# Linformer attention and gated feed-forward: small-matmul rounds joined, one block's softmax sums done in one round, loads of v and q reordered

## The chip, the cores and the metric

The kernel runs on one core of a Trainium2 chip. The metric is the device time of one execution in microseconds. The time before is 512.57 us (median of 4 runs, 511.74 to 514.13). Inputs are drawn at random in float32; the kernel works in bfloat16 with float32 sums.

## The reference

```python
# q, k, v: (batch 8, heads 8, seq 1024, dim 64); E, F: (64, 1024)
k_proj = einsum('ks,bhsd->bhkd', E, k)
v_proj = einsum('ks,bhsd->bhkd', F, v)
scores = q @ k_proj^T / 8
attn   = softmax(scores)                # over the 64 projected keys
x      = (attn @ v_proj), heads joined  # 8192 x 512
h      = x @ w_in                       # 512 -> 2048
out    = (h * sigmoid(1.702 h)) @ w_out # 2048 -> 512
```

## The kernel before

The kernel goes through 16 blocks of 512 rows of `x`. A block is 16 groups of 4 matmuls for `w_in` (`ffn1`) and 8 runs of 8 matmuls for `w_out` (`ffn2`). The attention of later blocks is pushed between them: `at(j, slot, f)` puts the work `f` behind slot `slot` of block `j`. There are 24 slots in a block and more in block 0, whose groups are halved; `O` is 16, the first run for `w_out`, and `Q` is the same place in block 0.

The attention matmuls are small. `eight` issues 64-row by 32-column matmuls that lie side by side in the array; I call one set of eight a round:

```python
def eight(outs, lhsTs, rhss):
    for i, ro in ((0, (LO, HI)), (1, (HI, LO))):
        for c in range(0, KP, 32):
            for ri, r in zip((LO, HI), ro):
                nc.tensor.matmul(outs[i][r.start + c:r.start + c + 32], lhsTs[i][ri, c:c + 32], rhss[i][ri], ...)
```

`scores` is one round and two exponentials on ScalarE. From block 4 on, the softmax sums of a block are one round (`sums`); VectorE inverts them, `spread` sends them out to DRAM and back over all partitions, and `values` (one round per half block) is multiplied by what came back. Block 3 is done by the older `norm`, which makes the sums anew on every partition, two rounds per half, and so needs no trip to DRAM:

```python
def norm(h, u):
    def go():
        e = [expT[h][:, 2 * u + i, :] for i in range(2)]
        d_ps = [ps_x.tile([P, TB], F32, name="x_ps") for _ in range(2)]
        eight(d_ps, [ones, ones], e)
        n_ps = [ps_x.tile([P, TB], F32, name="x_ps") for _ in range(2)]
        eight(n_ps, [vqs[h // NB2 % 2][:, 2 * u + i, :] for i in range(2)], e)
        for i in range(2):
            rd = att.tile([P, TB], F32, name="rdn")
            nc.vector.reciprocal(rd, d_ps[i])
            nc.vector.tensor_tensor(x_of(h)[:, 2 * u + i, :], n_ps[i], rd, op=ALU.mult)
    return go
```

`proj(b)` projects k and v of batch `b`; `load(b)` loads the batch from the GpSimd queue, in order, into single buffers:

```python
def load(b):
    load_kv(k, kt, b, "k_sb")
    if b == 1:
        load_kv(v, vt, b, "v_sb")
    load_q(b)                      # eight pieces
    if b > 1:
        load_kv(v, vt, b, "v_sb")
```

PSUM is split into two pools of four tiles: `f_ps` and `x_ps`.

The softmax here doesn't subtract the row's maximum and nothing guards it: scores larger than these inputs give would overflow.

## Time and profile before

| | before |
|---|---|
| time, median of 4 runs | 512.57 us |
| span of the profiled run | 510.4 us |
| TensorE busy | 504.4 us (99%), clock 1.000 |
| VectorE, ScalarE busy | 165.6 and 264.3 us |
| waits of TensorE | 2.7 us, all in the first 28 us |
| length of blocks 1, 2, 3 | 33.50, 34.78, 29.38 us |
| blocks 4 to 11, in turn | 31.02 and 29.16 us |

The length of a block is from the start of its first `w_in` group to that of the next block's, on TensorE's timeline. The lines of the profile are in the prediction.

### The profile page before, as it was taken

The numbers are of one execution on the slowest core, as the hardware profiler recorded it, in microseconds if no ns is written. First come the engines' busy times: TensorE is split into PE (matmuls) and PEld (weight loads), VectorE is DVE, ScalarE is ACT, GpSimd is POOL, SyncE is SP. The second block draws the span as 40 slices with busy tenths as digits, with TensorE's granted clock in tenths as the row PEclk, the third lists the DMA queues.
The fourth block names the chain that finished last, engine by engine and source line by source line (L and its number), as shares of the span: only waits on it lengthen the run. The fifth ranks groups of instructions, "written<-read, shape, count | busy, mean of one in ns | idle before, by whom it ended". The sixth has DMA issues, their size and how long they took to land.

```text
span 510.4 us, 7234 instructions
## 1 busy us (share of the span) xinstructions
PE 504.4 (99%) x3090; PEld 232.0 (45%) x3090; DVE 165.6 (32%) x221; ACT 264.3 (52%) x443; POOL 78.1 (15%) x97
## 2 busy tenths in 40 slices
PE   8999999999999999999999999999999999999997
PEld 4684444444444444444444444444444444444444
DVE  5513114765161623216161341616214161611000
ACT  2675564555637456471746637374563737244351
POOL 7442051514200051000510033000000000000000
PEclk9999999999999999999999999999999999999999
DMA  9999999999999099651998249990603205050202
GB/s 172 197 203 207 212 140 165 225 177 138 166 239 211 1 209 187 144 129 39 213 167 202 49 99 212 116 241 1 171 1 74 93 9 157 1 166 1 82 1 82
DMA packets 124752, 67.64 MB, mean 133 GB/s; under 512 B 92288, under 2 KB 116096, under 8 KB 122800
## 3 DMA queue, kind: packets, MB, share of 16 engines
q0 software_dynamic: 84400, 29.37, 51.4%
q1 hardware_dynamic: 40240, 37.56, 29.3%
q8 instruction: 24, 0.39, 0.3%
q10 hardware_dynamic: 80, 0.26, 0.2%
q14 instruction: 8, 0.07, 0.0%
HBM read 71.83 MB, written 16.97 MB: 174 GB/s over the span
## 4 chain that ended last, share of the span: by engine, by line
PE 94%; DMA 4%; POOL 1%; issue 0%; DVE 0%; ACT 0%; POOLq 0%
PE f_ps L405 43%; PE f_ps L373 43%; PE f_ps L165 3%; DMA w_in_sb<-in_moe_w_in_dram 2%; PE f_ps L262 2%; DMA v_sb<-in_v_dram 2%; PE x_ps L262 1%; PE x_ps L297 1%; POOL k_sb L57 0%; PE x_ps L359 0%; PE x_ps L344 0%; PE f_ps L397 0%; PE f_ps L244 0%; POOL q_sb L57 0%; POOL v_sb L57 0%
## 5 line engine op out<-in xcount | busy, mean ns | idle before, releaser
L405 PE MATMUL f_ps<-w_out_sb,gT 128*128 128x512 bf16 x1008 | 227.2, 379 | 0.0
L373 PE MATMUL f_ps<-xT,w_in_sb 128*128 128x512 bf16 (+1 forms) x1088 | 226.4, 367 | 0.3 <-DMA w_in_sb<-in_moe_w_in_dram 0.2
L376 ACT ACTIVATE gT<-f_ps 128x512 bf16<-128x512 f32 (+1 forms) x270 | 151.8, 574 | 61.4 <-PE f_ps L373 60.2
L373 PEld LDWEIGHTS <-w_in_sb 128*128 128x128 bf16 x1088 | 105.3, 98 | 116.2 <-issue 1.7
L405 PEld LDWEIGHTS <-gT 128*128 128x128 bf16 x1008 | 95.6, 98 | 120.5 <-issue 11.3
L408 ACT COPY o_sb<-f_ps 128x512 f32<-128x512 f32 x63 | 37.0, 587 | 126.8 <-PE f_ps L405 117.0
L332 DVE TENSOR_TENSOR xT<-x_ps,rbc 128x512 bf16<-128x512 f32 x48 | 30.9, 686 | 201.3 <-PE x_ps L262 124.9
L300 DVE RECIPROCAL rden<-x_ps 128x512 f32<-128x512 f32 x24 | 78.7, 3322 | 10.3 <-PE x_ps L297 10.3
L63 POOL DMA_DIRECT2D q_sb<-in_q_dram x56 | 49.1, 901 | 52.0 <-DMA k_sb<-in_k_dram 39.2
L278 ACT ACTIVATE expT<-f_ps 128x512 bf16<-128x512 f32 (+1 forms) x68 | 35.1, 571 | 32.7 <-PE f_ps L262 32.6
L57 POOL DMA_DIRECT2D k_sb<-in_k_dram x10 | 8.4, 846 | 175.5 <-PE f_ps L165 159.1
L219 DVE CAST k_b<-f_ps 64x512 bf16<-64x512 f32 x7 | 4.8, 683 | 46.8 <-PE f_ps L165 46.8
L278 ACT ACT_TABLE_LOAD x13 | 16.7, 1283 | 4.7 <-PE f_ps L262 4.5
L282 ACT ACT_TABLE_LOAD x14 | 18.0, 1283 | 0.2
L322 DVE RECIPROCAL rdn<-x_ps 128x512 f32<-128x512 f32 x4 | 13.4, 3353 | 0.8 <-PE x_ps L262 0.8
L165 PE MATMUL f_ps<-k_sb,eft 128*64 128x512 bf16 x56 | 13.4, 382 | 0.0
L165 PE MATMUL f_ps<-v_sb,eft 128*64 128x512 bf16 x56 | 13.4, 381 | 0.0
L399 DVE COPY o_sb<-f_ps 128x256 f32<-128x256 f32 x1 | 0.4, 424 | 38.6 <-issue 38.6
L135 PE MATMUL x_ps<-zeros 128*128 128x512 bf16 x34 | 11.2, 450 | 1.2 <-DVE zeros L106 1.2
L262 PE MATMUL f_ps<-qT,kt 64*32 64x512 bf16 x240 | 12.3, 386 | 0.0
L262 PE MATMUL x_ps<-expT,vq 64*32 64x512 bf16 x208 | 10.2, 377 | 0.0
L262 PEld LDWEIGHTS <-kt 64*32 64x32 bf16 x272 | 3.9, 88 | 13.7 <-issue 13.5
(71 smaller groups left out, 128.4 us busy)
## 6 DMA issues: line engine op xcount, KB each, us to landing
out_dram<-o_sb SPq DMA_DIRECT2D x15, 1024.0 KB
rbc<-rdr SPq DMA_DIRECT2D x24, 512.0 KB
k_sb<-in_k_dram POOLq DMA_DIRECT2D x7, 1024.0 KB, 13.3
v_sb<-in_v_dram POOLq DMA_DIRECT2D x7, 1024.0 KB, 10.6
q_sb<-in_q_dram POOLq DMA_DIRECT2D x56, 128.0 KB, 12.0
w_in_sb<-in_moe_w_in_dram POOLq DMA_DIRECT2D x8, 256.0 KB, 12.2
w_out_sb<-in_moe_w_out_dram POOLq DMA_DIRECT2D x4, 512.0 KB, 14.7
out_dram<-o_sb SPq DMA_DIRECT2D x3, 256.0 KB
```

Source lines behind the costliest of these rows:

```text
L63: nc.gpsimd.dma_start(out=qt[b][:, j], in_=qv[:, j])
L165: nc.tensor.matmul(kvps[b][r], eft(j, slice(e * KP, (e + 1) * KP)), (kt, vt)[e][b][:, :, j, :], start=(j == 0), stop=(j == J - 1))
L262: nc.tensor.matmul(outs[i][r.start + c:r.start + c + 32], lhsTs[i][ri, c:c + 32], rhss[i][ri], start=True, stop=True)
L278: nc.scalar.activation(expT[h][:, 2 * u + i, ts], s_ps[i], AF.Exp, scale=scale)
L282: nc.scalar.preload_act_table(AF.Gelu_apprx_sigmoid)
L300: nc.vector.reciprocal(rden[:, e, :], d_ps[e])
L322: nc.vector.reciprocal(rd, d_ps[i])
L332: nc.vector.tensor_tensor(x_of(h)[:, 2 * u + i, :], n_ps[i], rbc[h][:, 2 * u + i, :], op=ALU.mult)
L373: nc.tensor.matmul(h_ps, w_in_sb[:, kc, fc * P:(fc + 1) * P], xT[j][:, kc, ts], start=(kc == 0), stop=(kc == KC - 1))
L376: nc.scalar.activation(gts[j][:, fc, ts], h_ps, AF.Gelu_apprx_sigmoid)
L405: nc.tensor.matmul(o_ps[n], gts[j][:, fc, n * P:(n + 1) * P], w_out_sb[:, fc, :], start=(fc == 0), stop=(fc == FC - 1))
L408: nc.scalar.copy(osb[j][:, n, :], o_ps.pop(n))
```

## The change

It has three parts: the two halves of a score pair stand in one slot (the second half in the `x_ps` pool), block 3 goes over to `sums`, `spread` and `values` like the later blocks, and the loads are reordered. q of batch 2 goes into the buffer that batch 0 had to itself, apart from the one that the other batches share.

```diff
     def load(b):
-        load_kv(k, kt, b, "k_sb")
-        if b == 1:
-            load_kv(v, vt, b, "v_sb")
-        load_q(b)
-        if b > 1:
-            load_kv(v, vt, b, "v_sb")
+        for what in ("kvq", "kqv", "kvq", "qkv")[min(b, 4) - 1]:
+            ...
+    def q_buf(b):
+        t = ldpool.tile([P, J * H * D], BF16, name="q_even" if b in (0, 2) else "q_sb")
+        ...
-    def scores(h, u, half=None):
+    def scores(h, u, half=None, x=False):
...
-            s_ps = [f_tile([P, n * P]) for _ in range(2)]
+            s_ps = [(x_tile() if x else f_tile([P, TB]))[:, :n * P] for _ in range(2)]
...
-    at(0, 0, scores(0, 0, 1))
-    at(0, 1, scores(0, 1, 1), gelu_table)
+    at(0, 1, scores(0, 0, 1), scores(0, 1, 1, True), gelu_table)
...
-        at(0, Q + u, scores(1, u))
+        at(0, Q, scores(1, u, None, u > 0))
...
-        at(1, O + u, scores(2, u))
-        at(1, O + 3 + u, scores(3, u))
-        at(2, O + 2 * u, scores(4, u))
+        at(1, O, scores(2, u, None, u > 0))
+        at(2, O, scores(4, u, None, u > 0))
+        at(2, O + 3 * u, values(3, u))
...
-    at(1, O + 5, gelu_table)
+    for u in range(2):
+        at(1, O + 6, scores(3, u, None, u > 0))
+    at(1, O + 6, gelu_table)
...
-    at(2, 0, proj(2), kv_out(2))
-    at(2, 1, norm(3, 0))
-    at(2, 11, norm(3, 1))
+    at(2, 1, proj(2), kv_out(2), sums(3), spread(3))
     at(2, O, q_dma(3))
-    at(2, O + 4, scores(5, 0))
+    at(2, O + 3, scores(5, 0))
```

More of the change, by code (lines that the diff above doesn't have):

```diff
@@ L57, in load_kv @@
             nc.gpsimd.dma_start(out=dst[b][:, h:h + n, js:js + jn], in_=sv[:, h:h + n, js:js + jn])
+    def q_buf(b):
+        t = ldpool.tile([P, J * H * D], BF16, name="q_even" if b in (0, 2) else "q_sb")
+        order = "h j" if b == 0 else "j h"
+        return t.rearrange(f"p ({order} d) -> p {order} d", d=D, h=H)
     def load_q(b):
-        qt[b] = ldpool.tile([P, J, H, D], BF16, name="q_sb")
+        qt[b] = q_buf(b)
         qv = q[b].rearrange("h (p j) d -> p j h d", p=P)
@@ L65, in load @@
     def load(b):
-        load_kv(k, kt, b, "k_sb")
-        if b == 1:
-            load_kv(v, vt, b, "v_sb")
-        load_q(b)
-        if b > 1:
-            load_kv(v, vt, b, "v_sb")
+        for what in ("kvq", "kqv", "kvq", "qkv")[min(b, 4) - 1]:
+            if what == "q":
+                load_q(b)
+            elif what == "k":
+                load_kv(k, kt, b, "k_sb")
+            else:
+                load_kv(v, vt, b, "v_sb")
     w_in_v = moe_w_in.rearrange("(c p) f -> p c f", p=P)
@@ L85 @@
     make_identity(nc, ident)
-    load_kv(q, qt, 0, "q0_sb", H, 0, 2)
+    qt[0] = q_buf(0)
+    load_kv(q, qt, 0, "", H, 0, 2)
     load_kv(v, vt, 0, "v_sb", ((0, 4), (4, 2), (6, 2)))
-    load_kv(q, qt, 0, "q0_sb", H, 2, 2)
+    load_kv(q, qt, 0, "", H, 2, 2)
     for i in range(6):
         load_w_in(i)
-    load_kv(q, qt, 0, "q0_sb", H, JB, JB)
+    load_kv(q, qt, 0, "", H, JB, JB)
     for i in range(6, 8):
@@ L263, in eight, with x_tile @@
                                      start=True, stop=True)
-    def scores(h, u, half=None):
+    def x_tile():
+        return ps_x.tile([P, TB], F32, name="x_ps")
+    def scores(h, u, half=None, x=False):
         b, c = divmod(h, NB2)
```

## The prediction

> **What bounds the kernel now.** I read first the busy table of the page, then the list of what TensorE waited for, then TensorE's timeline, and last the timelines of VectorE and of the SyncE queue around block 2. (A block is 512 rows of the output; there are 16, numbered from 0. Each has 16 groups of four matmuls for the first weight matrix and 8 runs of eight for the second. I call these 24 places slots, and "slot 0 of the second half" is the first run of eight.)
>
> ```profile
> PE 504.4 (99%) x3090; PEld 232.0 (45%) x3090; DVE 165.6 (32%) x221; ACT 264.3 (52%) x443; POOL 78.1 (15%) x97
> PEclk9999999999999999999999999999999999999999
> ```
>
> TensorE is busy for 504.4 of 510.4 us at full clock; the other compute engines are idle for about half the time or longer. Busy matmuls are pipelined, so 99% alone could hide gaps. The waits of TensorE settle it:
>
> ```profile
> PE x_ps L135 <- DVE zeros L106: 1.2, 1, 1.2
> PE x_ps L359 <- DVE x_sb L351: 0.7, 1, 0.7
> PE f_ps L373 <- DMA w_in_sb<-in_moe_w_in_dram: 0.2, 1, 0.2
> ```
>
> These are the three longest of six, 2.7 us in all (columns: us in total, times, longest), and all six fall in the first 28 us. From there to the end TensorE never waits for anybody. So only fewer TensorE instructions, or less lost between them, can save time, and the change can only lose time by making a wait where there is none now. The timeline gives the price of each piece (columns: start, length, what, count):
>
> ```profile
> 71.07 1.89 PE L405 MATMUL f_ps<-w_out_sb,gT 128*128 128x512 bf16 x8
> 72.89 0.41 PE L262 MATMUL f_ps<-qT,kt 64*32 64x512 bf16 x8
> 73.23 1.90 PE L405 MATMUL f_ps<-w_out_sb,gT 128*128 128x512 bf16 x8
> ...
> 91.31 1.04 PE L373 MATMUL f_ps<-xT,w_in_sb 128*128 128x512 bf16 x4
> 92.28 0.41 PE L262 MATMUL x_ps<-expT,ones 64*32 64x512 bf16 x8
> 92.50 0.40 PE L262 MATMUL x_ps<-expT,vq 64*32 64x512 bf16 x8
> 92.83 8.81 PE L373 MATMUL f_ps<-xT,w_in_sb 128*128 128x512 bf16 x40
> ...
> 123.25 13.98 PE L373 MATMUL f_ps<-xT,w_in_sb 128*128 128x512 bf16 x64
> 137.07 1.89 PE L405 MATMUL f_ps<-w_out_sb,gT 128*128 128x512 bf16 x8
> 138.89 0.41 PE L262 MATMUL f_ps<-qT,kt 64*32 64x512 bf16 x8
> 139.11 0.40 PE L297 MATMUL x_ps<-expT,ones 64*32 64x512 bf16 x8
> 139.33 0.40 PE L262 MATMUL x_ps<-expT,vq 64*32 64x512 bf16 x8
> 139.66 10.53 PE L405 MATMUL f_ps<-w_out_sb,gT 128*128 128x512 bf16 x48
> ```
>
> Starts, not lengths, are to be compared. A full matmul costs (137.07 - 123.25)/64 = 0.216 us. Eight small ones (64 rows by 32 columns, all side by side in the array) are one round. An excursion from full matmuls to rounds and back costs, beyond its full matmuls: one round 73.23 - 71.07 - 8 x 0.216 = 0.43 us; two rounds 92.83 - 91.31 - 4 x 0.216 = 0.66; three 139.66 - 137.07 - 8 x 0.216 = 0.86. So a round is 0.215 us and **leaving and coming back costs 0.217 us** whatever is done there.
>
> **What the Trainium skill says.** "TensorEngine Tiling (Array Packing)", Key Properties: changing the tiling mode, not just the tile, drains TensorE. The trace agrees: the 0.217 us per excursion is two such changes. "TensorE: Matmul & The Clock Gate", Part 1, gives 215.7 ns from start to start for 512 columns; the trace has 216. So nothing is to be had from the full matmuls. "DMA: Bandwidth & Descriptors", Queues, rings and completion order: each DMA engine takes turns between the queues that have work. I use that for the share a small transfer gets beside the loads; the trace shows only the sum, loads and other traffic together at 195 GB/s from 92 to 106 us.
>
> **The change, part by part.**
>
> 1. Scores in one slot. The two halves of a block's scores now stand together, the second half writing to the other PSUM pool. Pairs joined: block 0's in the first slots, block 1's, block 2's, block 3's; each loses one excursion, 0.217 us. The joined pair in the first slots lies before 27.5 us, where TensorE waits for the weights' load anyway (the 0.2 us row), so I count it as nothing. Three pairs: 3 x 0.217 = 0.65 us saved. Block 4's pair I count with the next part.
>
> 2. Block 2. Before: two norm excursions of two rounds (2 x 0.656), block 4's two score excursions and block 5's first (3 x 0.432): 1.31 + 1.30 = 2.61 us. After: sums of block 3 behind the projection of batch 2; values and scores in one excursion of three rounds (0.86); values and scores in one of two (0.66). For work put behind a projection, the last such place of the trace tells: the projection alone cost 91.31 - 88.47 - 4 x 0.216 = 1.98, the projection with two rounds 121.52 - 115.55 - 16 x 0.216 = 2.51, so two rounds there cost 0.54, or 0.11 more than the rounds. One round: 0.32 us. Sum after: 0.32 + 0.86 + 0.66 = 1.84. Saved: 0.77 us.
>
> In the built order TensorE has eight matmuls fewer, as this says (norm 32; sums and values 24).
>
> 3. VectorE: four reciprocals of 3.35 us go and two of 3.32 come, 6.7 us less; the four products stay. It is busy 32% and was waited for nowhere in block 2: worth nothing by itself.
>
> 4. Loads. Batches 2 to 7 load the same bytes. From batch 4 on q comes first and waits for the transposes of the batch ahead, so q moves ahead of the k and v loads in steady state. All of it has some 50 us until it is used and TensorE waits for no load there: worth nothing.
>
> Sum: 0.65 + 0.77 = **1.42 us saved** on TensorE, 0.3%. 512.6 - 1.4 = 511.2.
>
> **Rivals.**
>
> (a) A new wait for the sums' round trip. Norm kept its sums on VectorE. Now block 3's reciprocals go out to DRAM and come back spread over partitions before its products can run. Block 4's trip in the kernel before shows how slow that is while loads run:
>
> ```profile
> 122.71 6.57 DVE L300 RECIPROCAL rden<-x_ps 128x512 f32<-128x512 f32 x2
> 129.31 0.62 SPq L307 DMA_DIRECT2D rdr<-rden  x1
> 134.75 1.35 SPq L310 DMA_DIRECT2D rbc<-rdr  x2
> 147.70 1.29 DVE L332 TENSOR_TENSOR xT<-x_ps,rbc 128x512 bf16<-128x512 f32 x2 [1.55 <-DMA rbc<-rdr]
> ```
>
> Reciprocals start 1.4 us behind the sums (two PSUM reads of the projection come first), the write out takes 5.4 us, the spread 12.9. In the changed kernel the sums of block 3 should end near 91.9 us, the reciprocals near 99.7, and the write, with the loads of batch 3 begun at 91.6, near 105. Were the spread as slow as that one, it would land at 118. I expect 114 to 118: by 105 the loads and the last output have moved 14 x 0.195 = 2.7 MB of 4.2 (four transfers of 1.05), 1.5 MB remain, and 1.05 MB of the spread taking turns with them is 2.1 MB at 195 to 255 GB/s, 8 to 11 us. Who waits? In the built order the sums of block 4 take the PSUM tiles that block 3's first products read, and stand at 121.19 - 1.42 = 119.8 us; two products take 1.29, so a landing after 118.5 stalls TensorE by the difference. For the rival: that margin is 0.5 to 4 us, the thinnest of the kernel. Against: v comes ahead of q now, so the projection of batch 3 is safe, and no output store falls beside this spread as one did at 136 us. If it strikes: 1 to 3 us lost, 511.5 to 514.
>
> (b) ScalarE at the end of block 1. Block 3's four exponentials (2 x 1.09), the table load (1.28) and an output copy (0.59) stand in a row where only two exponentials stood, 4.1 us from the scores, and ACT's first Gelu follows. TensorE's tiles for the next groups hang on these. But TensorE does scores, a run of eight, two groups and then the projection, 0.65 + 1.73 + 1.73 + 1.98 = 6.1 us, before it needs the copied tile. I give it no time. It would be worth 1 us at most.
>
> (c) The saving is hidden. It would be if TensorE waited for a transfer later; the list of waits has none after 28 us, so this holds for the first pair alone.
>
> (d) Steady state gains from spread loads. There is nothing on TensorE's path for that to shorten; 0. It may make the later spreads land sooner, unseen in the time.
>
> **Range and chances.** Without a stall 511.2; (a) strikes with a chance near one in five, for about 1.5 us, which adds 0.3 on average and stretches the upper side. I take 511.3. The three runs of before spread from 511.74 to 514.13, so the median itself is uncertain by about 1 us either way. Range 509.8 to 513.3. Two per cent is 10 us: no part is near it. Faster by over 2%: 0.01; within: 0.98; slower: 0.01.
>
> **What would show each step right or wrong.** TensorE's timeline: three-round and two-round excursions in block 2 at 0.86 and 0.66 us, no norm rounds, the start of block 3's groups (123.25 before) near 121.8. VectorE's first products of block 3: their start tells the landing; 114 to 118 as I say, and the sums of block 4 at 119.8 without a wait. TensorE's waits: still none after 28 us; one at the sums of block 4 or at block 3's first groups would be (a), one at the groups of block 2 (b). The second half of the trace: the same spacing, 13.82 us for 64 matmuls. The prediction is wrong if blocks 4 to 15 change length, or if block 2 holds a wait of over 2 us.

## The result

The changed kernel takes 511.33 us (median of 4 runs, 511.16 to 511.42). The ratio is 0.9972, with an interval from 0.9948 to 0.9996. Run again on another occasion (`after_again`), it gave 0.9974, from 0.9960 to 0.9987. That is 1.3 to 1.4 us, a change within 2%.

In the changed kernel's source the lines have moved: L271 is the rounds of `eight` (L262 before), L309 `sums` (L297), L385 and L417 the two feed-forward matmuls (L373 and L405), L174 the projection (L165). The page's first row, and then three of the six rows of what TensorE waited for (us in total, times, longest; the other three are 0.7, 0.2 and 0.2 us, also in the first 28 us):

```profile
PE 503.0 (99%) x3082; PEld 232.2 (46%) x3082; DVE 158.2 (31%) x219; ACT 263.8 (52%) x443; POOL 78.0 (15%) x97
```

```profile
PE x_ps L144 <- DVE zeros L115: 1.2, 1, 1.2
...
PE f_ps L385 <- ACT gT L388: 0.3, 1, 0.3
...
PE f_ps L385 <- DMA w_in_sb<-in_moe_w_in_dram: 0.2, 1, 0.2
```

Eight matmuls fewer, and still no wait after the first 28 us. The Gelu wait of 0.3 us is new; it lies at the very start. TensorE's timeline of block 2, from its first `w_in` group to that of block 3 (start, length, what, count; cut where `...` stands, and the last row ends with the view):

```profile
88.22 1.89 PE L385 MATMUL f_ps<-xT,w_in_sb 128*128 128x512 bf16 x8
...
91.89 0.41 PE L309 MATMUL x_ps<-expT,ones 64*32 64x512 bf16 x8
92.23 12.26 PE L385 MATMUL f_ps<-xT,w_in_sb 128*128 128x512 bf16 x56
104.33 1.89 PE L417 MATMUL f_ps<-w_out_sb,gT 128*128 128x512 bf16 x8
106.15 0.41 PE L271 MATMUL f_ps<-qT,kt 64*32 64x512 bf16 x8
106.37 0.40 PE L271 MATMUL x_ps<-expT,vq 64*32 64x512 bf16 x8
106.59 0.40 PE L271 MATMUL x_ps<-qT,kt 64*32 64x512 bf16 x8
106.92 5.35 PE L417 MATMUL f_ps<-w_out_sb,gT 128*128 128x512 bf16 x24
112.20 0.41 PE L271 MATMUL x_ps<-expT,vq 64*32 64x512 bf16 x8
112.43 0.40 PE L271 MATMUL f_ps<-qT,kt 64*32 64x512 bf16 x8
112.76 5.35 PE L417 MATMUL f_ps<-w_out_sb,gT 128*128 128x512 bf16 x24
...
120.12 0.40 PE L309 MATMUL x_ps<-expT,ones 64*32 64x512 bf16 x8
...
122.19 8.15 PE L385 MATMUL f_ps<-xT,w_in_sb 128*128 128x512 bf16 x37
```

Three rounds cost 106.92 - 104.33 - 8 x 0.216 = 0.86 us, two cost 112.76 - 106.92 - 24 x 0.216 = 0.66, as before. No norm round is left. The trip of block 3's sums, from VectorE's and the SyncE queue's timelines:

```profile
93.64 6.57 DVE L312 RECIPROCAL rden<-x_ps 128x512 f32<-128x512 f32 x2
100.24 0.62 SPq L319 DMA_DIRECT2D rdr<-rden  x1
104.87 1.32 SPq L322 DMA_DIRECT2D rbc<-rdr  x2
116.28 2.48 DVE L344 TENSOR_TENSOR xT<-x_ps,rbc 128x512 bf16<-128x512 f32 x4 [16.07 <-DMA rbc<-rdr]
```

The spread landed at 116.28 us; the second of the four products ended at 117.57 us, and the sums of block 4, which need the tiles of the first two, came at 120.12 us. So 2.5 us were left.

Where the time came from, by the lengths of the blocks:

| | before | changed | saved | predicted |
|---|---|---|---|---|
| block 0, second half | 16.50 | 16.27 | 0.23 | 0.22 |
| block 1 | 33.50 | 33.03 | 0.47 | 0.43 |
| block 2 | 34.78 | 33.97 | 0.81 | 0.77 |
| blocks 3 to 15 | 29.38, 31.02, 29.16 ... | 29.38, 31.01, 29.17 ... | 0.00 | 0 |
| sum | | | 1.51 | 1.42 |

The span fell by less, 510.4 to 509.6. The changed kernel's profiled run reached its first `w_in` group 0.44 us later (21.23 against 20.79). That is in a part that the change does not touch: over all profiled runs, the first group starts anywhere from 20.8 to 23.8 us. The rest belongs to the change. After the last copy on VectorE the program ran 3.0 us more in all ten profiled runs in which block 3's sums go through DRAM, and 2.7 us in the four with `norm`. At the end SyncE goes through nine waits for landed transfers, in a fixed order. With the three transfers of block 3's trip, 74 in place of 71 on that queue, the wait for the last store is the fourth of the nine and not the last, and the five behind it take 0.06 us each. So 0.3 of the 1.5 us is lost again at the end.

### The profile page after: what moved, and what is told of

Read it like the earlier page. It is cut to its first block, busy times and chain, and to the rows that moved or that the text cites. A ratio compares the mean times of both kernels' runs of the same rounds, so it can differ in the third digit from the quotient of the medians.

```text
span 509.6 us, 7212 instructions
## 1 busy us (share of the span) xinstructions
PE 503.0 (99%) x3082; PEld 232.2 (46%) x3082; DVE 158.2 (31%) x219; ACT 263.8 (52%) x443; POOL 78.0 (15%) x97
## 4 chain that ended last, share of the span: by engine, by line
PE 93%; DMA 4%; POOL 1%; issue 0%; DVE 0%; ACT 0%; POOLq 0%
PE f_ps L417 43%; PE f_ps L385 43%; PE f_ps L174 3%; DMA w_in_sb<-in_moe_w_in_dram 2%; DMA v_sb<-in_v_dram 2%; PE f_ps L271 2%; PE x_ps L271 1%; PE x_ps L309 1%; POOL k_sb L57 0%; PE x_ps L356 0%; PE x_ps L371 0%; PE f_ps L409 0%; PE f_ps L253 0%; POOL q_even L57 0%; POOL v_sb L57 0%
## 5 line engine op out<-in xcount | busy, mean ns | idle before, releaser
L417 PE MATMUL f_ps<-w_out_sb,gT 128*128 128x512 bf16 x1008 | 226.7, 379 | 0.0
L385 PE MATMUL f_ps<-xT,w_in_sb 128*128 128x512 bf16 (+1 forms) x1088 | 225.9, 367 | 0.7 <-ACT gT L388 0.3
L385 PEld LDWEIGHTS <-w_in_sb 128*128 128x128 bf16 x1088 | 105.5, 98 | 116.1 <-DMA w_in_sb<-in_moe_w_in_dram 0.9
L417 PEld LDWEIGHTS <-gT 128*128 128x128 bf16 x1008 | 95.9, 98 | 121.6 <-issue 11.8
L344 DVE TENSOR_TENSOR xT<-x_ps,rbc 128x512 bf16<-128x512 f32 x52 | 33.3, 684 | 217.5 <-PE x_ps L271 120.4
L312 DVE RECIPROCAL rden<-x_ps 128x512 f32<-128x512 f32 x26 | 85.3, 3322 | 10.4 <-PE x_ps L309 10.3
L70 POOL DMA_DIRECT2D q_sb<-in_q_dram x48 | 42.0, 905 | 151.1 <-DMA qT<-q_sb 122.3
L290 ACT ACTIVATE expT<-f_ps 128x512 bf16<-128x512 f32 (+1 forms) x58 | 30.1, 573 | 29.9 <-PE f_ps L271 29.9
L174 PE MATMUL f_ps<-k_sb,eft 128*64 128x512 bf16 x56 | 13.4, 382 | 0.0
L174 PE MATMUL f_ps<-v_sb,eft 128*64 128x512 bf16 x56 | 13.4, 382 | 0.0
L144 PE MATMUL x_ps<-zeros 128*128 128x512 bf16 x34 | 11.7, 469 | 1.2 <-DVE zeros L115 1.2
L271 PE MATMUL f_ps<-qT,kt 64*32 64x512 bf16 x208 | 10.6, 386 | 0.0
L271 PE MATMUL x_ps<-expT,vq 64*32 64x512 bf16 x208 | 10.2, 378 | 0.0
L363 DVE TENSOR_TENSOR x_sb<-x_ps,rd 128x256 bf16<-128x256 f32 x22 | 9.3, 424 | 0.8
L57 POOL DMA_DIRECT2D v_sb<-in_v_dram x10 | 8.4, 840 | 7.2 <-DMA q_sb<-in_q_dram 5.2
```

The source lines that it names most:

```text
L57: nc.gpsimd.dma_start(out=dst[b][:, h:h + n, js:js + jn], in_=sv[:, h:h + n, js:js + jn])
L70: nc.gpsimd.dma_start(out=qt[b][:, j], in_=qv[:, j])
L174: nc.tensor.matmul(kvps[b][r], eft(j, slice(e * KP, (e + 1) * KP)), (kt, vt)[e][b][:, :, j, :], start=(j == 0), stop=(j == J - 1))
L290: nc.scalar.activation(expT[h][:, 2 * u + i, ts], s_ps[i], AF.Exp, scale=scale)
L312: nc.vector.reciprocal(rden[:, e, :], d_ps[e])
L385: nc.tensor.matmul(h_ps, w_in_sb[:, kc, fc * P:(fc + 1) * P], xT[j][:, kc, ts], start=(kc == 0), stop=(kc == KC - 1))
```

## The experiments

Twelve more runs were made (one of them the changed kernel again), all with the right result. The table lists what each gave; the texts follow. Ratios are to the kernel before, in the same rounds. Only the intervals of block2_only, split_steady, q_ahead_of_v, after_again and first_split are clear of 1; for the rest the block lengths are the evidence, each from the one profiled run.

| run | median us (range) | ratio | block 2, us |
|---|---|---|---|
| pairs_only | 512.49 (512.40 to 512.97) | 0.9994 | 35.77 |
| block2_only | 518.96 (513.63 to 520.77) | 1.0106 | 41.21 |
| loads_only | 512.45 (512.06 to 513.35) | 0.9990 | 34.85 |
| split_steady | 513.80 (513.60 to 514.42) | 1.0020 | 33.96 |
| pairs_proj_later | 512.26 (511.89 to 513.28) | 0.9993 | 35.14 |
| q_ahead_of_v | 519.37 (515.01 to 520.65) | 1.0104 | 42.26 |
| sums_late | 513.17 (512.12 to 515.67) | 1.0014 | 35.00 |
| late_loads_old | 512.57 (511.04 to 513.73) | 0.9994 | 34.66 |
| after_again | 511.65 (510.96 to 512.22) | 0.9974 | 33.97 |
| v2_ahead | 513.90 (511.29 to 515.69) | 1.0016 | 35.47 |
| v2_ahead_tail | 512.61 (512.37 to 514.93) | 1.0005 | 35.47 |
| first_split | 511.81 (510.89 to 512.58) | 0.9978 | 33.97 |

### 1. Each part alone

The first three undo the two other parts. **pairs_only**: joined pairs, with block 2 and the loads as before.

> Only the joined score pairs of blocks 0 to 3; block 2 and the loads as in the kernel before. My theory (leaving the full matmuls and coming back costs 0.217 us each time, whatever is done there): in TensorE's timeline block 0's second half to block 1's first group is 0.22 us shorter than before, block 1 is 0.44 us shorter (33.50 before), block 2 keeps 34.78 and block 3 keeps 29.38 us; 0.65 us in all, after the first 28 us. Rival 1 (the gain comes from the eight matmuls fewer in block 2, and joined pairs only move work): nothing here, blocks 0 and 1 as before. Rival 2 (four exponentials in a row on ScalarE make TensorE wait): TensorE waits for ScalarE in block 1 or 2, and block 2 grows by up to 1 us. In the time, 512.6 to about 511.9, close to what the spread allows to be seen.

Measured: block 0's second half 16.28 and block 1 33.03 us, both as in the changed kernel, so rival 1 falls. But block 2 took 35.77 us, 0.99 more than before, and the gain was gone: ratio 0.9994. TensorE's timeline at the projection of batch 2 tells why, first of the kernel before, then of this run (the first matmul on k and the first on v):

```profile
89.42 0.40 PE L165 MATMUL f_ps<-k_sb,eft 128*64 128x512 bf16 x1
89.49 0.38 PE L165 MATMUL f_ps<-v_sb,eft 128*64 128x512 bf16 x1
```

```profile
88.87 0.40 PE L174 MATMUL f_ps<-k_sb,eft 128*64 128x512 bf16 x1
89.92 0.38 PE L174 MATMUL f_ps<-v_sb,eft 128*64 128x512 bf16 x1 [0.64 <-DMA v_sb<-in_v_dram]
```

At later projections v's first matmul starts in the same instant as k's. In the kernel before it was 0.07 us behind: v had landed just as it was needed. TensorE, now earlier, had to wait for it (v's first matmul stands 1.05 us behind k's). So rival 2 falls too (the wait is for a load), and my theory holds only for the saving, not for what came behind it.

**block2_only**: the sums of block 3 and the joined values, with pairs and loads as before.

> Only block 2's part (sums of block 3 behind the projection, values with the scores); pairs apart and loads as in the kernel before. My theory: block 2's length falls from 34.78 to about 34.0 us (0.77 to 0.81 less), blocks 0, 1 and 3 unchanged. Rival (the change of the loads is needed for it, because with q ahead of v the load of v of batch 3 now shares the DMA engines with the sums' spread and the projection of batch 3 waits for it): TensorE waits for the load of v or for the products of block 3 around 118 to 122 us, by 1 us or more, and the gain is lost. I expect the rival here at even odds. Time 511.8 without the wait, 512.5 to 514 with it.

The rival came true. TensorE waited 4.5 us for v of batch 3 and block 2 grew by 6.4 us (41.21 - 34.78). The loss is larger than expected (518.96 us against 512.5 to 514): the wait was longer than that allows for, and TensorE's clock fell after it, as in section 3. One of the six runs kept its clock at 1.0 and took 513.63 us.

**loads_only**: the new loads under the old schedule.

> Only the loads: q of batches 0 and 2 in a buffer of their own, v of batch 3 ahead of q, q first from batch 4; schedule of TensorE as before. My theory: nothing, every block's length as before to 0.05 us, no wait on TensorE after 28 us, time 512.6 plus or minus 0.5. Rival (the even, less crowded loads speed up the steady state or the change's gain comes from them): blocks 4 to 15 shorter than 30.2 and 29.2 us in turn, or the time down by 1 us or more.

As I expected: nothing (0.9990, interval 0.9977 to 1.0003; block 2 34.85, the others as before to 0.02). Of the three parts alone one is worth nothing, one loses its gain at once, and one costs over 1%. Together they save.

### 2. What an excursion costs

**split_steady** adds ten excursions to the changed kernel and not one matmul:

```diff
-                at(j, O + 6 * u, scores(j + 3, u))
+                at(j, O + (6 if u else 2), scores(j + 3, u))
```

> The changed kernel with the cost of an excursion added on purpose: in blocks 3 to 12 the first half of the scores moves two slots later, away from the values and sums it stood with. The same matmuls, ten excursions more. My theory: 10 x 0.217 = 2.2 us more than the changed kernel, each of the ten blocks 0.22 us longer; time about 513.5. Rival (the cost belongs to the small matmuls and not to the leaving and coming back, so that joining is worth nothing): the blocks as in the changed kernel, 511.3.

Blocks 3 to 12 came to 29.62, 31.24, 29.40, 31.24 us and so on, each 0.23 or 0.24 us longer; the ten sum to 301.58 against 299.26 us, 2.32 us in all. The time rose as it should, to 1.0020. The cost belongs to leaving the full matmuls and coming back. Small matmuls of the full mode (128 by 128, 130 columns) pay no such price: four of them take 0.22 to 0.23 us from their start to that of the next full matmul (48.89 to 49.12 us in the kernel before), which is what their 520 columns cost at the full matmuls' rate.

### 3. The order of the loads

**q_ahead_of_v** undoes one entry of the change, for batch 3:

```diff
-        for what in ("kvq", "kqv", "kvq", "qkv")[min(b, 4) - 1]:
+        for what in ("kvq", "kqv", "kqv", "qkv")[min(b, 4) - 1]:
```

> The changed kernel with one thing undone: batch 3 loads k, q, v again in place of k, v, q; the separate buffer for q of batches 0 and 2 stays. In the run with only block 2's part TensorE waited 4.5 us for v of batch 3 and then ran the projection at half clock. My theory (the order is the cause, because the last two q pieces may not be issued before earlier loads have landed, and v stands behind them): a wait of 3 to 6 us for v at the projection of batch 3, block 2 at 39 to 42 us, time 516 to 519. Rival (the shared q buffer is the cause, because q of batch 3 had to wait for the transposes of batch 2): no wait, block 2 at 34.0 us.

The order is a cause, and the shared q buffer is not: block 2 took 42.26 us. Shown in turn: TensorE's wait (a row of the list of waits), the GpSimd queue at the last q piece and v (with the idle time before and what ended it), and one row of the busy times by stretch (stretch, its length, then busy time of each engine; the third figure from the end is TensorE's clock):

```profile
PE f_ps L174 <- DMA v_sb<-in_v_dram: 5.9, 1, 5.9
```

```profile
106.62 0.88 POOL L70 DMA_DIRECT2D q_sb<-in_q_dram  x1 [7.05 <-DMA k_sb<-in_k_dram]
107.83 0.88 POOL L57 DMA_DIRECT2D v_sb<-in_v_dram  x1 [0.33 <-issue]
```

```profile
124.00:130.00 6.00, 5.31 (x36) 2.09 (x36) 1.63 (x4) 1.08 (x2) 0.81 (x1) 0.59 0.76 152
```

The queue is in order, and its eighth q piece may go out only when k has landed; v stood behind it and went out at 107.83 us, against 93.13 in the changed kernel. The order alone does not do it, though: in the kernel before, v of batch 3 went out as late (105.97 us) and landed 10.6 us later, ahead of its use. Here it took 16.8 us to land (124.65), in block2_only 15.9; what is new beside it is the spread of block 3's sums, which went out at 106.02 us. That the sharing slows it is argued from this, not tested by itself. The loss is larger than the wait: block 2 is 8.3 us longer for 5.9 us of wait. The rest is TensorE's clock, 0.59 from 124 to 130 us; the eight matmul pairs of the projection stand 0.43 us apart there, and 0.216 elsewhere. The Trainium skill has this in "TensorE: Matmul & The Clock Gate", Part 1: after an idle window of about 3.4 us the clock falls to one half. The run agrees; the wait of 1.4 us in v2_ahead (section 6) left the clock at 1.00. One of the four runs of q_ahead_of_v kept its clock (0.999) and took 515.01 us.

**late_loads_old** puts back the old order from batch 4 on (`"kqv"` for `"qkv"`).

> The changed kernel with the load order k, q, v from batch 4 on, as before; batches 2 and 3 as changed. My theory (nothing on TensorE hangs on it): blocks 2 to 15 as in the changed kernel to 0.02 us, time as there, 511.3 plus or minus 0.3. Rival (q first keeps the loads of batch 4 away from the spread of block 4's sums, which lands just in time): the first products of block 4 start after 147 us, against 145.0, and block 3 grows from 29.38 us.

Block 3 was 29.39 us and the later blocks as in the changed kernel; the first products of block 4 started at 145.74 us, against 145.00. The rival falls in this profiled run: that part of the change shortens no block. The time is less clear: the median is 512.57 us where 511.3 was expected, since two of the four runs took 513.5 and 513.7 us at a clock of 0.996 and 0.997, which no run of the changed kernel did. Only one of the shorter two was profiled. v2_ahead's profiled run has the same clock, 0.996, from a late start (0.66 from 10 to 15 us), so a late start may be the reason here too; it is not shown. But this run showed something else. Up to there it is the same program as the changed kernel, and yet block 2 took 34.66 us, because v of batch 2 was 0.73 us late (89.52 for k's first matmul, 90.25 for v's), and the products of block 3 started at 118.78 and not at 116.28. Both margins of block 2 are as small as what differs from run to run. In eight profiled runs with the pairs joined, the projection of batch 2 in slot 1 and q still ahead of v (that is the changed kernel and its repeat, pairs_proj_later, split_steady, q_ahead_of_v, sums_late, first_split and this one), v of batch 2 landed 0.04 to 0.72 us before k's first matmul in seven, and 0.7 us after it in this one.

### 4. The new trip of the sums

**sums_late** puts the sums of block 3 at slot 7 in place of slot 1.

> The changed kernel with the sums of block 3 six slots later (5.2 us), as an excursion of their own. This asks for rival (a) of the prediction. In the changed kernel the spread landed at 116.3 us and the sums of block 4, which reuse the tiles of block 3's first products, came at 120.1 us, 2.6 us after those products. If the reciprocals, the write, the spread and the products are the chain, the landing moves by 3 to 5 us and TensorE waits 0.5 to 2.5 us for a product of block 3 at the sums of block 4; block 2 at 34.6 to 36.6 us (0.11 of it for the excursion). If the chain is hidden in truth, 34.1 us and no wait.

VectorE's products and TensorE's sums of block 4, from the timelines:

```profile
119.45 2.48 DVE L344 TENSOR_TENSOR xT<-x_ps,rbc 128x512 bf16<-128x512 f32 x4 [15.59 <-DMA rbc<-rdr]
```

```profile
120.79 0.41 PE L309 MATMUL x_ps<-expT,ones 64*32 64x512 bf16 x7 [0.22 <-DVE xT L344]
```

The sums stood 4.9 us later, the landing was 3.2 us later than in the changed kernel, and TensorE waited for a product of block 3 just where the prediction's rival (a) said. Block 2 was 1.03 us longer: 0.11 for the separate excursion, 0.92 for the wait. The list says only 0.22, since the first of the eight matmuls ran in between. The mechanism is real; in the changed kernel it was short of striking by 2.5 us, in late_loads_old by 0.2 (second product done at 120.07, sums at 120.30).

### 5. Why the projection moved with the rest

**pairs_proj_later** is pairs_only with the projection of batch 2 in slot 1, as in the changed kernel.

> The run with only the joined pairs, and the projection of batch 2 one slot later (as in the changed kernel, but with norm and the old loads). My theory now (the pairs saved their 0.65 us, but TensorE then came to the projection of batch 2 before v of batch 2 had landed, and gave it all back): the 0.64 us wait for v goes, and block 2 is 34.78 or, with norm now right behind the projection and one change of mode fewer, about 34.67 us, in place of 35.77; blocks 0 and 1 as in the changed kernel; time about 511.9. Rival (block 2 is longer with the pairs joined for another cause, such as the four exponentials on ScalarE): block 2 stays near 35.8 us.

The wait for v went (both matmuls at 90.00 us), but block 2 was still 35.14 us. VectorE and TensorE around the second norm:

```profile
101.11 0.69 DVE L335 TENSOR_TENSOR xT<-x_ps,rdn 128x512 bf16<-128x512 f32 x1
```

```profile
101.14 0.41 PE L271 MATMUL x_ps<-expT,ones 64*32 64x512 bf16 x8
101.36 0.89 PE L271 MATMUL x_ps<-expT,vq 64*32 64x512 bf16 x8
102.19 3.63 PE L385 MATMUL f_ps<-xT,w_in_sb 128*128 128x512 bf16 x16
```

The second norm took 102.19 - 101.14 = 1.05 us where it took 0.56 before (101.57 to 102.13). It needs all four tiles of the pool, and the first norm's last product on VectorE ended only at 101.80 us. The first norm's reciprocals, 3.35 us each, had started 0.56 us later than before (93.59 against 93.03) because the projection did, while the second norm came 0.43 us earlier. The loss is 0.49 us, close to the excess over 34.67 us. So, for the whole gain, the pairs need the later projection, the later projection needs norm gone, and what replaces norm needs v of batch 3 early. Block 2's part with the new loads but without the joined pairs was not run.

### 6. Two attempts at more

**first_split** sets the first pair of scores apart again.

> The changed kernel with the very first pair of scores apart again. My prediction counted joining it as nothing, because TensorE waits for the weights there. Theory: the 0.3 us wait for a Gelu in the first slots goes, an excursion of 0.22 us comes back, and the groups behind the wait for the weights start at the same distance from the first group (6.72 us in the kernel before as in the changed one) to 0.1 us; block 2 and the rest as in the changed kernel.

Block 2 and the rest are unchanged, and the Gelu wait is gone. From the first `w_in` group to the first `w_out` run it took 17.41 us; the changed kernel took 17.35 in the repeat and 17.69 in the first profile, where the weights were waited for. The kernel before took 17.68, with that wait. In loads_only and block2_only, which start later and also have the first pair apart, it took 17.19 and 17.24. So joining the first pair shows no gain, and at most 0.2 us of loss (0.9978 against 0.9974).

**v2_ahead** loads v ahead of q for batch 2 too, to be rid of the late v.

> The changed kernel with v ahead of q for batch 2 as well. My theory (v of batch 2 lands at the very moment when it is needed, so luck decides up to 0.8 us): v is issued near 68 us in place of 79 and is there long before; block 2 is 33.97 us and the time is 0 to 0.7 us under the changed kernel. Rival (q of batch 2, now last, is late and its transposes hold up the queue on which the sums' spread and the transposes of k stand): the products of block 3 start after 119 us and TensorE waits in block 2, time up by 0.5 to 3 us.

v came early, and block 2 grew by 1.5 us: my theory fell and the rival was right. What came late for TensorE was the transposes of k, not the spread.

```profile
PE f_ps L271 <- DMA kt<-k_b: 1.4, 1, 1.4
```

```profile
92.47 5.06 SPq L261 DMA_TRANSPOSE qT<-q_even  x1
...
98.48 1.93 SPq L230 DMA_TRANSPOSE kt<-k_b  x1
```

The first row is TensorE's wait, the others are the SyncE queue. The last q piece of batch 2 now went out at 85.18 us (77.99 in the changed kernel), so its transposes held the queue to 97.5 us, where they had been done at 91.4, and the transposes of k stood behind them. Their result was not there when the scores of block 4 needed it. This run started late (first group at 23.8 us), which is part of the rise in its own time and of these later starts. The next run, with the usual start, had the same wait: the queue was held to 93.3 us against 91.4, the transposes of k went out 1.57 us later than in the changed kernel (94.31 against 92.74), and TensorE waited 1.43 us for them. So the changed kernel has little to spare there too.

**v2_ahead_tail** adds an earlier projection and joins the last two value rounds of the kernel.

> As the run before, with the projection of batch 2 and the sums of block 3 one slot earlier again (which v now allows, and which gives the spread 0.86 us more), and the last two value rounds of the kernel, for block 15, joined at the first excursion of block 14. One excursion fewer: block 13 goes from 28.74 to 28.3 us, block 14 from 28.07 to 28.3 us, together 0.217 us less; block 2 33.97. Time 0.2 us under the run before. If the theory of the excursion's cost is wrong, blocks 13 and 14 together stay at 56.81 us.

Block 2 had the same 1.4 us wait. But blocks 13 and 14 took 28.29 us each, 56.58 together, against 56.81: the joined rounds save 0.23 us. The changed kernel with this alone should be 0.2 us better; that one was not run.

## Why the prediction was right or wrong

- **The time**: 511.33 us, where 511.3 was told. The sum of the lengths, 1.51 us, is 0.09 above the 1.42 of the working, because leaving and coming back costs 0.23 and not 0.217 (block 1: 0.47 for two; split_steady: 2.32 for ten). The one-round excursion that I read started right behind a `w_in` group and gave 0.43; the others of that trace cost 0.44. The end of the program, for which I had no term, takes 0.3 us back. So the agreement to 0.03 us is luck: my two misses partly cancel, and the median of the kernel before (of four runs, not the three that I wrote) is itself uncertain by about 1 us.
- **Part 1, joined pairs**: right in size. The first pair was rightly counted as nothing, but not only for the reason given: where the weights are on time, a Gelu wait of 0.3 us takes its place (17.35 us joined, 17.41 apart), which I had not foreseen.
- **Part 2, block 2**: right, 0.81 for 0.77, each excursion within 0.02 us of the cost written.
- **Part 3, VectorE**: "worth nothing by itself" is right for the busy time. But pairs_proj_later shows that norm's reciprocals were near to being a wait: in the kernel before, the first norm's last product ended at 101.24 us and the second norm began at 101.57.
- **Part 4, loads**: this step failed as written: "All of it has some 50 us until it is used and TensorE waits for no load there: worth nothing". For the block lengths that holds from batch 4 on (late_loads_old). It does not for batches 2 and 3, whose v went out 10.7 and 13.1 us before its use in the kernel before (78.82 to 89.49, 105.97 to 119.11): v of batch 2 landed within 0.1 us of its use before the change, and without v ahead of q for batch 3 the changed schedule loses 8.3 us in block 2. I had named the second only in passing, under rival (a); the first not at all. The predicted time survived because the change moves the projection of batch 2 by one slot, 0.86 us, just more than the 0.70 us that TensorE gained ahead of it. For the prediction that was luck: I had not weighed it.
- **Rival (a)**: landing told as 114 to 118, measured 116.28; no stall, with 2.5 us left. The mechanism and the place are shown by sums_late.
- **Rival (b)**: right to give it no time; no wait for ScalarE in block 1 or 2.
- **Rivals (c) and (d)**: as told; blocks 3 to 15 are unchanged.

## What to carry to other kernels

When the busiest engine has no waits left, joining small work of another array shape is worth the number of times it leaves and comes back, and that price can be read from two places of the timeline. An empty list of waits does not say how near the next wait is: look at what landed just in time, and expect that a gain ahead of it is lost there unless the load or its user moves too. Test the parts of such a change alone: here no part saved anything by itself.

## What the Trainium skill lacked or had wrong

- "TensorEngine Tiling (Array Packing)", Key Properties, says that a change of the mode drains TensorE, but not what it costs: 0.23 us for leaving and coming back (2.32 us for ten).
- "TensorE: Matmul & The Clock Gate", Back-to-back issue gap, gives about 131 ns per matmul of 512 columns, each with its own weight load, as the sustained rate, and calls 216 ns too high. In these runs 64 such pairs took 13.82 us, 216 ns each, in all blocks.
- "DMA: Bandwidth & Descriptors", Anatomy of one DMA, fits 2.0 us plus bytes over 436 GB/s, which is 4.4 us for the 1.05 MB written by a load of v, or 6.8 us for the 2.10 MB of float32 that it reads (estimates from that fit). Beside other loads, v of batch 2 took 10.6 us from issue to landing in ten of the twelve profiled runs that load it behind q, and 11.7 us in the other two (block2_only, late_loads_old). The page has no figure for several loads of one core that share the engines.
- "DMA: Bandwidth & Descriptors" has a bandwidth for DMA transposes and sequencer cycles for one large case, but not how long a DMA transpose of 1.05 MB holds the queue that issues it beside other traffic: 5.0 to 12.6 us in the changed kernel (at 121.50 and 153.02 us), with all later transfers of that queue behind it.
